# Block-sparse attention and feed-forward kernel: the scores of a row of blocks in two matrix products instead of three, and staging loads in order of use

## The chip, the cores and the metric

The kernel runs on one core of a Trainium2 chip. The metric is the device time of one execution in microseconds. Before the change the median of three runs is 852.0 us (850.26 to 855.06).

## What is computed

Block-sparse attention for 4 batches, 8 heads, 768 positions of 64 elements, and behind it a feed-forward layer with an ELU on the joined heads. A block is 32 positions, so a sequence has 24 blocks. A query sees its own block and both neighbours, the first and the last block, and three sampled blocks; queries of the first and the last block see everything.

```
scores = scale * np.matmul(q, k.transpose(0, 1, 3, 2))
mask = np.abs(blk_i - blk_j) <= 1
mask = mask | (blk_i == 0) | (blk_j == 0) | (blk_i == n_blocks - 1) | (blk_j == n_blocks - 1)
...
attn = np.exp(scores - max); attn = attn / (sum + 1e-09); x = attn @ v
h = x @ w_in
g = np.where(h > 0.0, h, np.exp(np.minimum(h, 0.0)) - 1.0)
out = g @ w_out
```

Inputs q, k and v are float32, the weights float64.

## The kernel before, in words

**Number format.** Every operand of a product is held as a high and a low float16 part, and each product is three float16 products (`PROD`: high x high, high x low, low x high) summed in PSUM.

**Units.** The 22 inner blocks of a batch form six units: `u` 0 to 4 hold four query blocks (`QB`), `u` 5 holds two and, as the "special" rows, the first and the last block. Each unit is done for half of the heads at a time (`qd` 0 and 1; `u` 5 in one go), which makes 11 score units a batch and 44 in all. For each query block a score row has 256 columns (`ROW`): 96 of the window, 32 of the first block, 96 of the sampled blocks, 32 of the last block.

**Scores** (`scores`, L438 to L457). For each head pair half `pp`, each of the three products and each of three parts, there are eight products, four query blocks by two heads. A product takes 64 rows and 32 columns of the array, so the eight cover it. Part 0 reads the window from `kT` (96 columns), part 1 the first and last keys from `kE` (64 columns), part 2 the sampled keys from `kR` (96 columns). A unit is 2 x 3 x 3 x 8 = 144 products, each with its own weight load. `gather_k` (L413 to L420) copies the sampled key blocks of a unit into `kR`, 12 copies on VectorE, whose places it reads from registers; `kR` has one buffer. `ends_of_k` (L370 to L376) fills `kE` once a batch.

**Behind the scores.** `sm_min` (VectorE, with the mask) and `sm_exp` (ScalarE), a step later `sm_hi` and `sm_lo`, then the transpose by DMA on SP's queue (`sm_T`, L500), `attn_v` (L513) four or six steps behind the scores, `norm` (L533) and `turn_x` (transposes on TensorE, L325, and a split into `xT` by ScalarE and VectorE, L313 and L316). The tile `vg` holds the V rows of a unit: the window by SP's queue and the sampled ones by GpSimd's (`gather_v`, L408 and L409), the first and last block by `edge_v` (L400).

**PSUM.** Scores, special scores and the transposes of k, q and x take turns in two buffers (`ps_s`, tag "s"). The special scores take both at once (`sp_scores`, L549) until the exponential (`spt`, L567) is done.

**Feed-forward.** A chunk `t` is two units of a batch, 256 tokens; there are 12. `ffn_h` (L629) is 24 products of 256 columns a step, eight steps a chunk; `ffn_o` (L664) is 12 products of 512 columns a step, eight steps.

**Order.** A table of steps sets the order: `st.at(step, rank, fn)` puts a piece of work in a step, and the pieces are emitted step by step and by rank. A scheduler behind it may still move instructions. Chunk `t` has its feed-forward part at steps 12 + 16t to 28 + 16t; its attention begins 22 steps (`LEAD`) ahead, for chunks 0 and 1 closer. One step of the later chunks is 24 or 12 feed-forward products on TensorE plus, in most steps, a piece of attention. Weights are converted from float64 in 32 pieces by ScalarE, VectorE and GpSimd at steps 2 to 23 (`w_bits1`, `w_sign`, `w_bits2`, `w_split`).

**Staging.** q, k and v of a later chunk or batch come through a ring of three buffers (`st`, `NST`): `load_q`, `load_k`, `load_v` on SP's queue, then `turn_k`, `turn_q` (transposes on TensorE) or `prep_v_hi`, `prep_v_lo` (ScalarE, VectorE), which give the buffer back. Before the change a load of k or v stands two steps ahead of its use, a load of q three; the pieces of k of the next batch are used at steps e0 + 2 + 6n and those of v at e0 + 16 + 4n (n from 0 to 5, e0 the step where the batch's attention begins); for batch 1 they are used at steps 22 to 34, every second step.

Of the kernel before, what the change touches and what calls it, by code (L numbers as in the profile page):

```python
# [7 lines left out]
F32 = mybir.dt.float32  # L8
F16 = mybir.dt.float16
# [5 lines left out]
BLOCK = 32  # L15
# [23 lines left out]
def kernel(  # L39
# [22 lines left out]

    nc = tc.nc
    B, H, S, D = q.shape
    P = 128
# [14 lines left out]
    NFP = NFC // 2  # L82
    CW = 2 * P
    assert D == 64 and NR == 3 and NB == 24 and H == 8

    QS, KS, VS = -2.0, 16.0, 32.0
    SS = 2.0 ** 8
# [73 lines left out]
    mask = const.tile([P, NU, 8], F32, tag="mask", name="mask")  # L161

    def build_mask():
        tb = const.tile([P, 6, 8], F32, tag="tb", name="tb")
# [24 lines left out]
        nc.vector.tensor_scalar(nv[:, 7:8], pq, float(NB - 2), None, op0=ALU.is_equal)  # L189
# [79 lines left out]
    vg = [const.tile([P, 2, QB, H * 2 * D], F16, tag=f"vg{i}", name=f"vg{i}") for i in range(2)]  # L269
    vN = const.tile([P, NK, H, 2, D], F16, tag="vN", name="vN")  # L270
    scr = {}
    kT, qT, kR, kE, stg, nat = {}, {}, {}, {}, {}, {}

    def spare(i, n, m=1):

# [92 lines left out]
                  ps[:, d, 0:P].rearrange("p (a i) -> p a i", a=2), 1.0)  # L368

    def ends_of_k(b):  # L370

        t = work.tile([P, 2 * NPAIR, 2, BLOCK], F16, tag="kE", bufs=1, name=f"kE{b}")
        kE[b] = t
        for e, s0 in enumerate((0, S - BLOCK)):
            nc.vector.tensor_copy(
                t[:, :, e, :], kT[b].rearrange("p l a s -> p (l a) s")[:, :, s0 : s0 + BLOCK])  # L376
# [19 lines left out]
    slot = {}  # L396

    def edge_v(b, s, eng=None):
        for ab, s0 in ((0, 0), (1, S - BLOCK)):
            (eng or nc.sync).dma_start(  # L400
                vg[s][96:P, ab],
                scr[b][s0 : s0 + BLOCK].rearrange("i (o e) -> i o e", o=1).to_broadcast(
                    [BLOCK, QB, H * 2 * D]))

    def gather_v(b, u, i):
        qb = 1 + QB * u + i
# [4 lines left out]
            in_offset=bass.IndirectOffsetOnAxis(ap=rix[0:96, qb : qb + 1], axis=0))  # L411

    def gather_k(b, u):  # L413

        t = work.tile([P, 2 * NPAIR, QB * NR, BLOCK], F16, tag="kR", bufs=1, name=f"kR{b}_{u}")
        kR[b, u] = t
        kk = kT[b].rearrange("p l a s -> p (l a) s")
        for c in range(blocks_in(u) * NR):
            x = token_of(1 + QB * u + c // NR, c % NR)
            nc.vector.tensor_copy(t[:, :, c, :], kk[:, :, bass.ds(x, BLOCK)])  # L420

    def blocks_in(u):
        return QB if u < UL else 2
# [12 lines left out]
    def scores(b, u, qd):  # L436
        ps = ps_s.tile([P, 2, 2, ROW], F32, tag="s", name=f"s{b}_{u}_{qd}")
        pS[b, u, qd] = ps  # L438
        for pp in range(2):
            for ql, kl in PROD:  # L440
                for part in range(3):
                    for n, (d, i, q0) in enumerate(places(u, qd)):
                        a, s0 = 2 * d + pp, BLOCK * (QB * u + i)
                        for j in range(2):
                            js = slice(64 * j, 64 * j + 64)
                            o = ps[32 * n : 32 * n + 32, j, pp, :]
                            if part == 0:
                                o, m = o[:, 0:96], kT[b][js, kl, a, s0 : s0 + 96]
                            elif part == 1:
                                o = o.rearrange("p (a k) -> p a k", a=2)[:, :, 96:128]  # L450
                                m = kE[b][js, kl * NPAIR + a]
                            else:
                                o = o[:, P : P + 96]
                                m = kR[b, u][js, kl * NPAIR + a, NR * i : NR * (i + 1)]
                            nc.tensor.matmul(  # L455
                                o, lhsT=qT[b, u][js, ql, a, q0 : q0 + 32], rhs=m,
                                start=(ql + kl + part == 0), stop=(ql == 1),  # L457
                                skip_group_check=True)

# [234 lines left out]
    def unit(s, b, u, qd, t, c0):  # L694
        lag = 4 if t == 1 else 6
        if qd == 0:
            st.at(s - (3 if t else 1), 3.0, lambda: gather_k(b, u))
        st.at(s, 0, lambda: scores(b, u, qd))
        st.at(s, 5, lambda: sm_min(b, u, qd))
        st.at(s, 6, lambda: sm_exp(b, u, qd))  # L700
        if t == 0:
            st.at(s + 1, 0.5, lambda: turn_p(b, u, qd))
            st.at(s + 2, 1, lambda: attn_v(b, u, qd))
            if qd == 1:
                st.at(s + 2, 3.5, lambda: norm(b, u))
                st.at(s + 3, 0.6, lambda: turn_x(b, u, t, c0))
            return
        st.at(s + 1, 3.1, lambda: sm_hi(b, u, qd))
        st.at(s + 1, 3.2, lambda: sm_lo(b, u, qd))
        st.at(s + 2, 0.5, lambda: sm_T(b, u, qd))  # L710
        a = s + lag
        st.at(a, 1, lambda: attn_v(b, u, qd))
        if u == UL or qd == 1:
            st.at(a, 3.5, lambda: norm(b, u))
            st.at(a, 7, lambda: turn_x(b, u, t, c0))

    def special(s, b, qd, t):
        st.at(s, 0, lambda: sp_scores(b, qd))
# [8 lines left out]
        if qd == NQ - 1:  # L727
            st.at(s + lag, 3.5, lambda: sp_x(b, t, P))

    def k_piece(s, b, c):  # L730
        st.at(s - 2, 0.1, lambda: load_k(b, c))
        st.at(s, 7.2, lambda: turn_k(b, c))

    def v_piece(s, b, g, qd):
        st.at(s - 2, 0.1, lambda: load_v(b, g, qd))
        st.at(s, 3.6, lambda: prep_v_hi(b, g, qd))
        st.at(s, 3.7, lambda: prep_v_lo(b, g, qd))
        if qd == NQ - 1:
            st.at(s + 1, 0.8, lambda: store_v(b, g))

    PIECES = [(g, qd) for g in range(NG) for qd in range(NQ)]
    for t, (b, us) in enumerate(chunks):
# [22 lines left out]
        for m, u in enumerate(us):  # L765
            s = first[m]
            if t == 0:
                continue
            st.at(s - 6, 0.1, lambda b=b, u=u: load_q(b, u))
            st.at(s - 3, 7.1, lambda b=b, u=u: turn_q(b, u))  # L770

        opens = t == 0 or chunks[t - 1][0] < b
        for m, u in enumerate(us):
# [103 lines left out]
```

## Time and profile before

| | |
|---|---|
| median of three runs | 852.0 us |
| the profiled execution, its own time | 850.52 us |
| its span on the core | 848.8 us |
| TensorE products | 716.1 us busy (84%), 15,111 instructions, as many weight loads |
| VectorE, ScalarE, GpSimd | 473.2, 390.9, 270.5 us busy |
| mean granted clock of TensorE | 0.925 |
| score products | three groups of 2,112 |

The profile is of one execution. Busy times overlap, and a share of the whole span mixes stages with different limits, so stretches of the span are read apart. A row of waits names the engine, the tile and the line that waited, what ended the wait, the total in us, how often, and the longest. "issue" means that the profile shows no releaser. A timeline row has start, duration, engine, line, tiles, shapes and count, and in brackets the idle time ahead of it.

### The profile page before, as it was taken

To read this page: it belongs to the slowest core of one execution; us is meant where nothing else is said; L and a number is where in the kernel's file an instruction comes from. 1 tells how busy PE (TensorE), PEld (TensorE's weight loads), DVE (VectorE), ACT (ScalarE), POOL (GpSimd) and SP (SyncE) were. 2 spreads that over 40 slices of the span, in tenths; PEclk is the share of its full clock that TensorE was granted. 3 is DMA by queue.
4 is the path that set the end of the run, shared out by engine and by line. 5 is a ranking of instruction groups with operands and counts; after the bars stand their busy time and mean duration, and the time that the engine had idled before them with its cause. 6 is when DMAs were issued, how large, how long until landed. Compare 5 with 4: busy or idle time off the path is not lost. (4 is left out here: it accounts for less than half of the span.)

```text
span 848.8 us, 34525 instructions
## 1 busy us (share of the span) xinstructions
PE 716.1 (84%) x15111; PEld 497.2 (59%) x15111; DVE 473.2 (56%) x1247; ACT 390.9 (46%) x830; POOL 270.5 (32%) x249
## 2 busy tenths in 40 slices
PE   2355367579699799799899899899999999999998
PEld 2244345337566666666655656757757758567583
DVE  3838789984564664553624664464736635445040
ACT  3542465554543554543534553454635535445140
POOL 1438567730411411412410410421422304213040
PEclk9656759869899899989999999999999999999999
DMA  9995555878749858538638847546868555353000
GB/s 213 319 211 176 162 142 165 200 154 215 179 89 186 157 120 182 127 83 170 126 55 194 162 107 174 128 108 146 141 142 176 86 90 125 47 133 49 29 2 25
DMA packets 204938, 116.59 MB, mean 137 GB/s; under 512 B 163060, under 2 KB 183668, under 8 KB 204788
## 3 DMA queue, kind: packets, MB, share of 16 engines
q1 hardware_dynamic: 191952, 88.89, 50.1%
q0 software_dynamic: 5952, 18.36, 8.4%
q10 hardware_dynamic: 6884, 7.15, 2.8%
q8 instruction: 118, 1.93, 1.0%
q14 instruction: 32, 0.26, 0.1%
HBM read 74.52 MB, written 12.58 MB: 103 GB/s over the span
## 5 line engine op out<-in xcount | busy, mean ns | idle before, releaser
L629 PE MATMUL h<-xT,wih 128*128 128x256 f16 x1536 | 271.4, 282 | 16.3 <-issue 6.2
L664 PE MATMUL o<-woh,g 128*128 128x512 f16 x768 | 242.1, 383 | 5.6 <-ACT woh L263 3.6
L654 POOL TENSOR_TENSOR g<-e,g 128x512 f16<-128x512 f32 x96 | 113.7, 1184 | 364.6 <-DVE g L651 330.4
L629 PE MATMUL h<-xT,wil 128*128 128x256 f16 x768 | 216.3, 282 | 3.1 <-issue 3.1
L664 PEld LDWEIGHTS <-g 128*128 128x128 f16 x1152 | 109.5, 98 | 139.2 <-issue 19.3
L629 PEld LDWEIGHTS <-wih 128*128 128x128 f16 x1536 | 151.5, 101 | 41.5 <-issue 17.5
L664 PE MATMUL o<-wol,g 128*128 128x512 f16 x384 | 147.2, 383 | 6.7 <-POOL wol L264 5.6
L481 ACT ACTIVATE t<-t,m 128x256 f32<-128x256 f32 x176 | 87.3, 497 | 117.1 <-DVE m L466 113.3
L409 POOL DMA_INDIRECT vg<-scr,rix x88 | 84.4, 959 | 133.6 <-PE av L513 113.7
L647 DVE SCALAR_TENSOR_TENSOR e<-h,e 128x512 f32<-128x512 f32 x96 | 66.2, 689 | 72.2 <-ACT e L643 69.3
L466 DVE CUSTOM_DVE_ANT_1 t<-s,mask 128x256 f32<-128x256 f32 x176 | 64.4, 419 | 57.9 <-PE s L455 56.1
L637 ACT ACTIVATE e<-h 128x512 f32<-128x512 f32 x96 | 56.5, 588 | 72.7 <-PE h L629 65.4
L455 PEld LDWEIGHTS <-qT 64*32 64x32 f16 x6336 | 56.5, 91 | 57.1 <-issue 43.5
L629 PEld LDWEIGHTS <-wil 128*128 128x128 f16 x768 | 77.6, 101 | 16.0 <-POOL wx L244 3.1
L493 DVE SCALAR_TENSOR_TENSOR p<-t,p 128x1024 f16<-128x1024 f32 x40 | 48.7, 1218 | 40.4 <-ACT p L488 40.2
L643 ACT ACTIVATE e<-e,gs 128x512 f32<-128x512 f32 x96 | 69.2, 721 | 2.2
L455 PE MATMUL s<-kE,qT 64*32 64x64 f16 x2112 | 57.4, 201 | 15.0 <-issue 11.9
L455 PE MATMUL s<-kR,qT 64*32 64x96 f16 x2112 | 60.8, 215 | 9.3 <-issue 6.7
L455 PE MATMUL s<-kT,qT 64*32 64x96 f16 x2112 | 56.5, 216 | 14.4 <-DVE m L466 10.0
L420 DVE COPY kR<-kT 128x256 f16 x264 | 50.3, 249 | 6.3 <-issue 4.4
L513 PEld LDWEIGHTS <-pT 128*32 128x32 f16 x4224 | 42.6, 98 | 18.7 <-issue 16.2
L513 PE MATMUL av<-vg,pT 128*32 128x64 f16 x4224 | 49.0, 202 | 4.2 <-DMA vg<-scr 3.0
(102 smaller groups left out, 727.3 us busy)
## 6 DMA issues: line engine op xcount, KB each, us to landing
vg<-scr SPq DMA_DIRECT2D x88, 192.0 KB, 5.9
wk<-in_moe_w_out_dram SPq DMA_DIRECT2D x16, 512.0 KB, 3.8
wk<-in_moe_w_in_dram SPq DMA_DIRECT2D x12, 512.0 KB, 4.2
scr<-vN SPq DMA_DIRECT2D x12, 512.0 KB, 4.4
out_dram<-r ACTq DMA_DIRECT2D x20, 256.0 KB, 4.0
stq<-in_q_dram SPq DMA_DIRECT2D x18, 256.0 KB, 4.3
stv<-in_v_dram SPq DMA_DIRECT2D x18, 256.0 KB, 4.2
stk<-in_k_dram SPq DMA_DIRECT2D x18, 256.0 KB, 3.6
```

Source lines behind the costliest of these rows:

```text
L409: nc.gpsimd.indirect_dma_start(out=t[0:96, 1, i], out_offset=None, in_=scr[b], in_offset=bass.IndirectOffsetOnAxis(ap=rix[0:96, qb : qb + ...
L420: nc.vector.tensor_copy(t[:, :, c, :], kk[:, :, bass.ds(x, BLOCK)])
L455: nc.tensor.matmul(o, lhsT=qT[b, u][js, ql, a, q0 : q0 + 32], rhs=m, start=(ql + kl + part == 0), stop=(ql == 1), skip_group_check=True)
L466: nc.vector.tensor_tensor_reduce(t[:, j, pp, :].rearrange("p (a b) -> p a b", b=BLOCK), ps[:, j, pp, :].rearrange("p (a b) -> p a b", b=BL ...
L481: nc.scalar.activation(t[:, j, pp, :], t[:, j, pp, :], AF.Exp, bias=m[:, j, pp : pp + 1], scale=-1.0, accum_out=s[:, h : h + 1])
L513: nc.tensor.matmul(o[32 * n : 32 * n + 32, 4 * qd + 2 * pp + j, :], lhsT=t[:, pl * 8 + (2 * j + pp) * 2 + ab, 32 * n : 32 * n + 32], rhs=v ...
L629: nc.tensor.matmul(ps[:, e, :], lhsT=w[2 * f + e][:, cs], rhs=x[:, l, cc, :], start=(n == 0), stop=(n == 3 * NCC - 1))
L637: nc.scalar.activation(e, hS[t, f], AF.Exp, scale=IH)
L643: nc.scalar.activation(e, e, AF.Relu, bias=gs_col, scale=-GS)
L647: nc.vector.scalar_tensor_tensor(e, hS.pop((t, f)), -IH * GS, e, op0=ALU.mult, op1=ALU.min)
L654: nc.gpsimd.tensor_tensor(gl[f], eS.pop((t, f)), gh[f], op=ALU.subtract)
L664: nc.tensor.matmul(o, lhsT=g[f][:, e, ms], rhs=w[2 * f + e], start=(f == 0 and e == 0 and n == 0), stop=(f == NFP - 1 and e == 1 and n == 2))
```

## The change

- **Two products a row.** `kE` is gone. `kR` is one lasting tile with 17 key blocks in a row: first, three sampled, last, three sampled, first, three sampled, last, three sampled, first. A query block's second product reads five blocks in a row (160 columns) from there: an end, its three sampled blocks, and the other end. For odd query blocks of a unit the last key block comes first and the first one last. So columns 96 to 256 of a row hold the ends in turns, and a unit has 96 products, 48 of 96 columns and 48 of 160.
- **Ends.** `ends_of_k` writes the first keys to three places and the last keys to two, in two copies of 768 and 512 elements a partition. The mask's column for a doubled end moves to match.
- **Edge V.** The end rows of `vg` follow the same order, so `edge_v` issues four DMAs of half the size instead of two: on GpSimd's queue for batch 0 (8 for 4), on SP's for the others (24 for 12).
- **`turn_x`** stands one step later for all chunks but chunk 0.
- **Staging.** Loads are sorted by the step of their use; each is put at the end of a step (rank 9), six steps ahead or at the step in which the third load before it is used, if that is later. For batch 1 that gives leads of two to six steps, from then on always six.
- **K and V pieces** of batches 2 and 3 are used at other steps (K at e0 + 11, 15, 23, 31, 39, 41, V at e0 + 17, 19, 25, 27, 33, 35), none of K between the special scores and their end.
- **`gather_k`** for the first unit of chunk 2 stands one step ahead of its scores instead of three.
- The mask's scratch tile comes from a pool of work tiles.

```diff
-    kT, qT, kR, kE, stg, nat = {}, {}, {}, {}, {}, {}
+    kT, qT, stg = {}, {}, {}
+    kR = const.tile([P, 2 * NPAIR, QB * (NR + 1) + 1, BLOCK], F16, tag="kR", name="kR")
...
     def ends_of_k(b):
-        t = work.tile([P, 2 * NPAIR, 2, BLOCK], F16, tag="kE", bufs=1, name=f"kE{b}")
-        kE[b] = t
-        for e, s0 in enumerate((0, S - BLOCK)):
+        for e, s0 in ((0, 0), (NR + 1, S - BLOCK)):
+            t = kR[:, :, e :: 2 * (NR + 1), :]
             nc.vector.tensor_copy(
-                t[:, :, e, :], kT[b].rearrange("p l a s -> p (l a) s")[:, :, s0 : s0 + BLOCK])
+                t, kT[b].rearrange("p l a s -> p (l a) s")[:, :, s0 : s0 + BLOCK].unsqueeze(2)
+                .to_broadcast([P, 2 * NPAIR, t.shape[2], BLOCK]))
...
     def edge_v(b, s, eng=None):
-        for ab, s0 in ((0, 0), (1, S - BLOCK)):
-            (eng or nc.sync).dma_start(
-                vg[s][96:P, ab],
+        for ab in range(2):
+            for i in range(2):
+                s0 = (S - BLOCK) * (ab ^ i)
+                (eng or nc.sync).dma_start(
+                    vg[s][96:P, ab, i::2],
...
-                for part in range(3):
+                for part in range(2):
...
                             if part == 0:
-                                o, m = o[:, 0:96], kT[b][js, kl, a, s0 : s0 + 96]
-                            elif part == 1:
-                                o = o.rearrange("p (a k) -> p a k", a=2)[:, :, 96:128]
-                                m = kE[b][js, kl * NPAIR + a]
+                                c, m = slice(0, 96), kT[b][js, kl, a, s0 : s0 + 96]
                             else:
-                                o = o[:, P : P + 96]
-                                m = kR[b, u][js, kl * NPAIR + a, NR * i : NR * (i + 1)]
+                                e = (NR + 1) * i
+                                c, m = slice(96, ROW), kR[js, kl * NPAIR + a, e : e + NR + 2]
...
-            st.at(s - (3 if t else 1), 3.0, lambda: gather_k(b, u))
+            st.at(s - (1 if t == 0 or s == F0 + 2 * NSTEP - LEAD else 3), 3.0, lambda: gather_k(b, u))
...
-            st.at(a, 7, lambda: turn_x(b, u, t, c0))
+            st.at(a + 1, 7, lambda: turn_x(b, u, t, c0))
...
+    def q_piece(s, b, u):
+        staged.append((s, lambda: load_q(b, u)))
+        st.at(s, 7.1, lambda: turn_q(b, u))
...
     def k_piece(s, b, c):
-        st.at(s - 2, 0.1, lambda: load_k(b, c))
+        staged.append((s, lambda: load_k(b, c)))
...
-                    k_piece(e0 + 2 + 6 * n, b + 1, n)
-                    v_piece(e0 + 16 + 4 * n, b + 1, g, qd)
+                    k_piece(e0 + (11, 15, 23, 31, 39, 41)[n], b + 1, n)
+                    v_piece(e0 + (17, 19, 25, 27, 33, 35)[n], b + 1, g, qd)
...
+    staged.sort(key=lambda it: it[0])
+    for n, (s, load) in enumerate(staged):
+        st.at(max(s - 6, staged[n - NST][0] if n >= NST else 0), 9, load)
```

TensorE's order where batch 2's second chunk turns its normalised rows (`xt_0` of unit 0, behind a piece `h_4` of the feed-forward part of the chunk before), in the kernel before:

```order
L629 LDWEIGHTS wil_1483
L629 MATMUL h_4_11581<-xT_10021,wil_1483 128x256
L325 MATMUL xt_0_11617<-ident,xf_0_11614 128x128 x4
L325 MATMUL kt_4_11624<-ident,stk_4_11398 128x128 x4
L629 LDWEIGHTS wih_1486
L629 MATMUL h_5_11631<-xT_10021,wih_1486 128x256
```

And now:

```order
L632 LDWEIGHTS wil_1314
L632 MATMUL h_5_10257<-xT_8887,wil_1314 128x256
L331 MATMUL xt_0_10292<-ident,xf_0_10255 128x128 x4
L457 LDWEIGHTS qT_1_9765
L457 MATMUL s_1_1_10301<-kT_5052,qT_1_9765 32x96
```

`xt_0` stood behind `h_4` and had a transpose of k (`kt_4`) right behind it; now it stands behind `h_5`, right ahead of the scores `s_1_1`, and the transpose of k is elsewhere.

SP's queue behind the special scores of batch 2 (`spT`: transposes of the special rows, `pT`: of the others, `stv`, `stk`, `stq`: staging loads, `scr`: V written out, `vg`: V gathered), before:

```order
L588 DMA_TRANSPOSE spT_1_1_10033<-spp_1_1_10014 128x12x128
L293 DMA stv_0_1_10724<-in_v_dram 128x4x128
L500 DMA_TRANSPOSE pT_5_0_10422<-p_5_0_10407 128x16x128
L288 DMA stk_3_10726<-in_k_dram 128x8x64
L306 DMA stq_1_10728<-in_q_dram 128x8x64
L392 DMA scr_11051<-vN 128x2048
L293 DMA stv_1_0_11089<-in_v_dram 128x4x128
L288 DMA stk_4_11398<-in_k_dram 128x8x64
L500 DMA_TRANSPOSE pT_0_0_10730<-p_0_0_10721 128x16x128
```

And now:

```order
L591 DMA_TRANSPOSE spT_1_1_8854<-spp_1_1_8843 128x12x128
L299 DMA stv_0_0_9007<-in_v_dram 128x4x128
L299 DMA stv_0_1_9206<-in_v_dram 128x4x128
L503 DMA_TRANSPOSE pT_5_0_9210<-p_5_0_9195 128x16x128
L312 DMA stq_1_9326<-in_q_dram 128x8x64
L294 DMA stk_2_9466<-in_k_dram 128x8x64
L397 DMA scr_9712<-vN 128x2048
L299 DMA stv_1_0_9611<-in_v_dram 128x4x128
L299 DMA stv_1_1_9773<-in_v_dram 128x4x128
L503 DMA_TRANSPOSE pT_0_0_9468<-p_0_0_9460 128x16x128
```

Pieces 3 and 4 of k stood here, with pieces of v one by one; now it is piece 2 of k, and the pieces of v come in pairs.

More of the change, by code (lines that the diff above doesn't have):

```diff
@@ L84 @@
     assert D == 64 and NR == 3 and NB == 24 and H == 8
+    assert (NB - 3) % QB % 2 == 1
     QS, KS, VS = -2.0, 16.0, 32.0
@@ L163, in build_mask @@
     def build_mask():
-        tb = const.tile([P, 6, 8], F32, tag="tb", name="tb")
+        tb = work.tile([P, 6, 8], F32, tag="e", bufs=NE, name="tb")
         sf, df, t0, t1 = (tb[:, i, :NR] for i in range(4))
@@ L188, in build_mask @@
         nc.vector.tensor_scalar(nv[:, 3:4], pq, 1.0, None, op0=ALU.is_equal)
-        nc.vector.tensor_scalar(nv[:, 7:8], pq, float(NB - 2), None, op0=ALU.is_equal)
+        nc.vector.scalar_tensor_tensor(
+            nv[:, 3:4], pq, float(NB - 2), nv[:, 3:4], op0=ALU.is_equal, op1=ALU.add)
         nb = const.tile([P, 8], BF16, tag="nb", name="nb")
@@ L398, in edge_v @@
     def edge_v(b, s, eng=None):
-        for ab, s0 in ((0, 0), (1, S - BLOCK)):
-            (eng or nc.sync).dma_start(
-                vg[s][96:P, ab],
-                scr[b][s0 : s0 + BLOCK].rearrange("i (o e) -> i o e", o=1).to_broadcast(
-                    [BLOCK, QB, H * 2 * D]))
+        for ab in range(2):
[3 more added lines that the diff above has]
+                    vg[s][96:P, ab, i::2],
+                    scr[b][s0 : s0 + BLOCK].rearrange("i (o e) -> i o e", o=1).to_broadcast(
+                        [BLOCK, QB // 2, H * 2 * D]))
     def gather_v(b, u, i):
@@ L413, in gather_k @@
     def gather_k(b, u):
-        t = work.tile([P, 2 * NPAIR, QB * NR, BLOCK], F16, tag="kR", bufs=1, name=f"kR{b}_{u}")
-        kR[b, u] = t
         kk = kT[b].rearrange("p l a s -> p (l a) s")
-        for c in range(blocks_in(u) * NR):
-            x = token_of(1 + QB * u + c // NR, c % NR)
-            nc.vector.tensor_copy(t[:, :, c, :], kk[:, :, bass.ds(x, BLOCK)])
+        for i in range(blocks_in(u)):
+            for r in range(NR):
+                x = token_of(1 + QB * u + i, r)
+                nc.vector.tensor_copy(
+                    kR[:, :, (NR + 1) * i + 1 + r, :], kk[:, :, bass.ds(x, BLOCK)])
     def blocks_in(u):
@@ L445, in scores @@
                             js = slice(64 * j, 64 * j + 64)
-                            o = ps[32 * n : 32 * n + 32, j, pp, :]
                             if part == 0:
-                                o, m = o[:, 0:96], kT[b][js, kl, a, s0 : s0 + 96]
-                            elif part == 1:
-                                o = o.rearrange("p (a k) -> p a k", a=2)[:, :, 96:128]
-                                m = kE[b][js, kl * NPAIR + a]
-                            else:
-                                o = o[:, P : P + 96]
-                                m = kR[b, u][js, kl * NPAIR + a, NR * i : NR * (i + 1)]
+                                c, m = slice(0, 96), kT[b][js, kl, a, s0 : s0 + 96]
+                            else:
+                                e = (NR + 1) * i
+                                c, m = slice(96, ROW), kR[js, kl * NPAIR + a, e : e + NR + 2]
                             nc.tensor.matmul(
-                                o, lhsT=qT[b, u][js, ql, a, q0 : q0 + 32], rhs=m,
+                                ps[32 * n : 32 * n + 32, j, pp, c],
+                                lhsT=qT[b, u][js, ql, a, q0 : q0 + 32], rhs=m,
                                 start=(ql + kl + part == 0), stop=(ql == 1),
@@ L728, in special @@
             st.at(s + lag, 3.5, lambda: sp_x(b, t, P))
+    staged = []
+    def q_piece(s, b, u):
+        staged.append((s, lambda: load_q(b, u)))
+        st.at(s, 7.1, lambda: turn_q(b, u))
     def k_piece(s, b, c):
-        st.at(s - 2, 0.1, lambda: load_k(b, c))
+        staged.append((s, lambda: load_k(b, c)))
         st.at(s, 7.2, lambda: turn_k(b, c))
     def v_piece(s, b, g, qd):
-        st.at(s - 2, 0.1, lambda: load_v(b, g, qd))
+        staged.append((s, lambda: load_v(b, g, qd)))
         st.at(s, 3.6, lambda: prep_v_hi(b, g, qd))
@@ L768 @@
                 continue
-            st.at(s - 6, 0.1, lambda b=b, u=u: load_q(b, u))
-            st.at(s - 3, 7.1, lambda b=b, u=u: turn_q(b, u))
+            q_piece(s - 3, b, u)
         opens = t == 0 or chunks[t - 1][0] < b
```

## The prediction

> **What bounds the kernel now.** I read the page first, then the stretches with the busy time of each engine, then the waits of TensorE in the two stretches that matter, then the timeline of one score unit.
>
> ```profile
> span 848.8 us, 34525 instructions
> PE 716.1 (84%) x15111; PEld 497.2 (59%) x15111; DVE 473.2 (56%) x1247; ACT 390.9 (46%) x830; POOL 270.5 (32%) x249
> q8 instruction: 118, 1.93, 1.0%
> ```
> ```profile
> core 0: us, PE busy (x) PEld busy (x) DVE busy (x) ACT busy (x) POOL busy (x), PEclk, DMA share, GB/s
> 23.00:80.00 57.00, 25.17 (x1011) 20.03 (x1010) 40.02 (x108) 25.01 (x57) 30.00 (x29) 0.64 0.87 238
> 80.00:196.00 116.00, 73.92 (x1474) 47.62 (x1473) 98.34 (x172) 61.90 (x122) 72.62 (x54) 0.76 0.68 171
> 196.00:650.00 454.00, 418.13 (x9064) 292.06 (x9065) 242.54 (x701) 215.79 (x469) 115.75 (x109) 0.97 0.67 141
> 650.00:848.80 198.80, 191.50 (x3529) 131.44 (x3527) 82.58 (x228) 79.91 (x167) 48.82 (x45) 1.00 0.36 70
> ```
>
> The kernel has two regimes. Up to 196 us TensorE is busy for less than two thirds of a stretch: first the opening attention, then the conversion of the weights on VectorE (98 of 116 us), GpSimd and ScalarE. Behind 196 us TensorE is busy for 610 of 653 us and the next engine for half: what shortens TensorE's work or removes a wait of its own moves the end. Its waits from 196 us on (total, times, longest):
>
> ```profile
> PE xt L325 <- DVE xf L533: 11.8, 5, 6.9
> PE h L629 <- issue: 9.3, 6, 3.3
> PE kt L325 <- ACT spt L567: 7.8, 2, 4.9
> PE s L455 <- issue: 6.3, 8, 1.3
> PE o L664 <- issue: 2.6, 2, 1.6
> PE av L513 <- issue: 0.5, 1, 0.5
> ```
>
> That is 19.6 us for buffers and data (`xt`, `kt`) and 18.7 us of "issue", waits for which the profile shows no releaser.
>
> **The scores, part by part.** The start of one unit at 194.63, and the next unit whole, between products of the feed-forward part (start, duration):
>
> ```profile
> 194.63 0.24 PE L455 MATMUL s<-kT,qT 64*32 64x96 f16 x8 [0.55 <-DVE kT L316]
> ...
> 208.58 0.24 PE L455 MATMUL s<-kT,qT 64*32 64x96 f16 x8
> 208.63 0.21 PE L455 MATMUL s<-kE,qT 64*32 64x64 f16 x8
> 208.66 0.23 PE L455 MATMUL s<-kR,qT 64*32 64x96 f16 x8
> 208.71 0.23 PE L455 MATMUL s<-kT,qT 64*32 64x96 f16 x8
> ...
> 209.62 0.26 PE L455 MATMUL s<-kE,qT 64*32 64x64 f16 x8
> 209.69 0.27 PE L455 MATMUL s<-kR,qT 64*32 64x96 f16 x8
> 209.89 0.39 PE L629 MATMUL h<-xT,wih 128*128 128x256 f16 x2
> ```
>
> Eighteen groups of eight products, each product with a weight load of its own, take 1.31 us. From the first group to the last there are 17 intervals in 1.11 us, 0.065 us each, and late in the unit 64 columns (kE to kR) take the same 0.07 us as 96 do. Only the first groups, which had queued up, follow at 0.05, 0.03, 0.05 us, by their width. So a group costs about 0.065 us for its sixteen instructions, and its columns about 0.03 us per 64. The change leaves twelve groups: six of 96 columns and six of 160. By instructions alone 11 intervals are 0.72 us, plus the 0.20 us to the next product: 0.92, a saving of 0.39. If a wide group costs its columns, 160/64 x 0.03 = 0.075 us, it is 6 x 0.065 + 5 x 0.075 = 0.77, plus 0.20 and 0.03 for a longer last group: 1.00, a saving of 0.31. I take 0.35. Of 44 units nine lie ahead of 196 us or so (four of chunk 0, three of chunk 1, two of chunk 2, whose second is the one at 194.63); 35 x 0.35 = **12 us** (11 to 14).
>
> A rule of the Trainium skill speaks against it (TensorE: Matmul & The Clock Gate, The mechanism): a weight load overlaps a running product only if it goes to another row group. By it the four places of one half of the rows would run one after another, and wider products would cost more than fewer save. Here four 96-column products in a row would need 4 x 0.05 = 0.20 us and a whole group starts every 0.065 us, so the trace doesn't bear the rule out; it is a rival below.
>
> **The waits for xt and kt.** The two stalls for `kt` are transposes of K that stand behind the special scores, which hold both buffers until the exponential is done; no piece of K stands there any more: 7.8 us go. The stalls for `xt` come from VectorE, which does the normalisation behind pieces of V that have not landed. Over the same stretch ScalarE waits:
>
> ```profile
> ACT vN L313 <- DMA stv<-in_v_dram: 39.8, 11, 5.7
> ```
> ```profile
> 226.28 1.11 PE L325 MATMUL xt<-ident,xf 128*128 128x128 f32 x4 [6.88 <-DVE xf L533]
> 227.19 1.06 PE L325 MATMUL kt<-ident,stk 128*128 128x128 f32 x4
> 228.04 0.63 PE L629 MATMUL h<-xT,wih 128*128 128x256 f16 x2
> 228.47 0.42 PE L629 MATMUL h<-xT,wil 128*128 128x256 f16 x1
> ```
>
> Now `turn_x` stands a step later, behind one more piece of 24 products. From batch 1's chunks on, each load is issued six steps ahead. So the four later stalls, 11.8 - 6.9 = 4.9 us, go. The one at 226 us lies where K and V of batch 1 are loaded; there three staging buffers leave leads of two to four steps as before. It shrinks by one step (24 products at 0.11 us, from the 0.43 us below halved to 0.22 per two, 2.6 us) to some 4.2. What is late next at these places is the split of `xt_3`: on VectorE it stands behind the low part of `p_4_1`, and the special scores need its buffer. I allow 1 us at each of three places, **3 us** (0 to 6). Sum: 7.8 + 4.9 + 2.6 - 3 = **12 us**.
>
> Each such stall also leaves TensorE at half clock (granted clock 0.97 on average from 196 to 650 us, 1.00 after): after it two `h` products take 228.47 - 228.04 = 0.43 us, where 0.22 is the rate of undisturbed stretches:
>
> ```profile
> 208.16 0.38 PE L629 MATMUL h<-xT,wih 128*128 128x256 f16 x2
> 208.38 0.27 PE L629 MATMUL h<-xT,wil 128*128 128x256 f16 x1
> ```
>
> I estimate 1 to 2 us lost behind each of the four stalls of 2.8 us or more; with most of them gone, **4 us**.
>
> **The issue waits.** The instruction queue brought 1.93 MB in 118 packets, and 2 x 15,111 instructions of TensorE are most of what is fetched: 1.93 MB / 30,222 is 64 bytes each, so one 16 KB packet is about 256 instructions. A unit's 288 instructions are more than one packet in 1.3 us; 192 are less. TensorE has 4,224 instructions fewer in all (14%). I take half of the 18.7 us, **10 us** with some clock (bounds: 3 by the 14%, 24 if all go). The Trainium skill says the opposite (Runtime: NRT & Kernel Launch, Instruction fetch mechanics): crossing such a block is mostly hidden. By it this term is nothing; that is a rival too.
>
> **The opening.** From 23 to 80 us:
>
> ```profile
> PE s L455 <- issue: 12.7, 3, 5.3
> PE s L455 <- DVE kE L375: 3.1, 1, 3.1
> PE av L513 <- DMA vg<-scr: 3.0, 1, 3.0
> ```
>
> Three stalls inside the score units hold VectorE's minima and everything queued behind them, the weights too. With 384 instructions fewer there I take **5 us** (0 to 12). Against it: the end copies are wider, and edge V takes twice as many issues.
>
> ```profile
> L375 DVE COPY kE<-kT 128x256 f16<-128x256 f16 x8 | 1.5, 215 | 0.0
> ```
> ```profile
> L400 POOL DMA_DIRECT2D vg<-scr x4: 581/604/802, 35.2 to 39.8; - x4
> ```
>
> The copies carry 768 and 512 elements for 256: between 215 ns each and 3 and 2 times that, so 0 to 0.65 us a batch. Only the first pair is waited for (kE, above); elsewhere VectorE is busy for half the time. Four more issues of GpSimd are 2.4 us ahead of its gathers, half of them ahead of the first `av`; twelve more on SP, at that price, are 7 us over the run, with no engine waiting for SP's queue in the lists above. I charge 1 us, inside the 5. The mask takes as many small operations as before, and its scratch tile only comes from another pool: nothing.
>
> **The sum.** 12 + 12 + 4 + 10 + 5 = 43 us, against the profiled execution's own 850.5 us (848.8 of span and 1.7 around it): 807.5. That execution lay 1.5 us under the median of the runs shown, 852.0, so I forecast **809 us** (main case 798 to 821).
>
> **The rivals.**
> - Issue waits stay, because fetches are bound by other traffic, in the opening too: 850.5 - 12 - 12 - 4 = 822.5, as a median **824**. For it: the waits fall on `h` and `o` as well, where instructions are sparse. Chance 0.17.
> - The `xt` and `kt` stalls come back elsewhere, since three staging buffers are all there is: 850.5 - 12 - 10 - 5 = 823.5, **825**. Against it: from 650 us, where no K and V are loaded, none is left. 0.10.
> - The edit doesn't do what it says: a 160-column group costs as much as the two it replaces, and only the order gains: 850.5 - 12 - 4 - 10 - 5 = 819.5, **821**. 0.05.
> - All stalls go: 14 for the scores, 19.6 and 4, 24, 10: 779, **780**. 0.08.
> - Slower: loads on SP. A load that waits for a staging buffer holds the transposes of p behind it, and `av` waits for those.
>
> ```profile
> SPq L308 <- PE kt L325: 16.3, 3, 10.2
> ```
> ```profile
> 304.46 3.42 SPq L500 DMA_TRANSPOSE pT<-p  x1
> 317.80 1.01 PE L513 MATMUL av<-vg,pT 128*32 128x64 f16 x96
> ```
> ```profile
> pT<-p SPq DMA_TRANSPOSE x40, 5.5
> ```
>
> The transpose lands 5.5 us after issue and has 317.8 - 304.5 = 13.3, so 7.8 us cover a held queue. The longest hold seen is 10.2; if each of the 22 units of batches 1 and 2 met it, 2.4 x 22 = 53 us would come on top: 807.5 + 53, as a median **862**. It ends above the present time from holds of 9.8 us at every unit. Against it: six steps ahead, the buffer has been given back by the load's place in the program. 0.04.
> - Slower: the places of one row half run one after another. A unit is 6 x 4 x (0.05 + 0.075) = 3.0 us, 1.7 more than now; 35 x 1.7 = 59 us for a saving of 12: 807.5 + 12 + 59, **880**. The trace refutes it for today's widths. That is what the rule of the Trainium skill named above (TensorE: Matmul & The Clock Gate, The mechanism) would do. 0.02.
>
> **How the numbers follow.** The main case has 0.54. The range 788 to 831 takes it in with the first three rivals, and leaves out the fast end and both slow cases, 0.14, and some of the main case's tail. A measurement of this kernel can tell 0.5%, about 4 us, from no change: faster by more than that are the main case and the first four, 0.92, less some for unforeseen stalls: 0.90; the slow cases and those, 0.06; the rest 0.04.
>
> **What would show it.** In the changed profile: 96 products a unit, first to next `h` in 0.9 to 1.0 us; no `kt` wait on `spt`, the `xt` waits under 6 us; issue waits of TensorE behind the opening about half of 18.7; the three stalls of the opening under 8 us together. The prediction is wrong if units take over 1.1 us, if `av` waits for transposes, or if the special scores wait for `xt_3` by more than 2 us each.

## The result, and the profile after

| | kernel before | changed kernel |
|---|---|---|
| median of the runs | 851.2 us (850.26 to 855.06, 4 runs) | 790.67 us (788.61 to 794.8, 4 runs) |
| the profiled execution, its own time | 850.52 us | 794.8 us |
| its span | 848.8 us | 792.7 us |
| mean granted clock of TensorE | 0.925 | 0.931 |

The changed kernel takes 0.9285 of the time [0.9254, 0.9316]: 60 us less, where 43 were forecast. The head of the page, with the instruction queue, and the two groups that are left of the scores:

```profile
span 792.7 us, 30338 instructions
PE 693.7 (88%) x12999; PEld 480.9 (61%) x12999; DVE 480.4 (61%) x1247; ACT 387.7 (49%) x830; POOL 272.9 (34%) x253
q8 instruction: 102, 1.67, 0.9%
L457 PE MATMUL s<-kT,qT 64*32 64x96 f16 x2112 | 45.5, 217 | 20.8 <-issue 8.1
L457 PE MATMUL s<-kR,qT 64*32 64x160 f16 x2112 | 48.7, 250 | 5.8 <-DVE kR L425 5.0
```

TensorE lost 2,112 products and as many weight loads, and 22 us of busy time; the span lost 56 us. So most of the gain was idle time of TensorE. The stretches show where (each row: window, its length, then busy time and instructions of PE, PEld, DVE, ACT and POOL, granted clock, DMA share, GB/s):

```profile
23.00:80.00 57.00, 25.80 (x828) 19.51 (x827) 38.71 (x110) 25.04 (x57) 32.80 (x33) 0.61 0.84 235
80.00:190.00 110.00, 75.66 (x1242) 47.82 (x1241) 101.31 (x178) 62.87 (x125) 73.56 (x54) 0.74 0.69 182
190.00:600.00 410.00, 396.21 (x7789) 278.03 (x7788) 245.94 (x698) 211.69 (x467) 113.30 (x108) 0.99 0.70 155
600.00:792.70 192.70, 188.78 (x3110) 129.75 (x3107) 84.79 (x224) 79.86 (x168) 49.94 (x46) 1.00 0.36 74
```

Behind 190 us TensorE is now busy for 585 of 603 us, where it was 610 of 653, and its granted clock in the long stretch rose from 0.97 to 0.99. Its waits from 190 us to the end (total, times, longest):

```profile
PE xt L369 <- DVE xf L536: 4.5, 2, 2.7
PE s L457 <- DVE xT L322: 2.6, 2, 1.4
PE h L632 <- DVE e L650: 2.1, 1, 2.1
PE h L632 <- issue: 1.6, 1, 1.6
PE kt L331 <- DVE kT L322: 1.1, 1, 1.1
PE s L457 <- DVE kR L379: 0.5, 1, 0.5
PE xt L331 <- DVE xf L536: 0.5, 1, 0.5
PE sp L552 <- DVE xT L322: 0.4, 2, 0.2
PE av L516 <- issue: 0.3, 1, 0.3
PE s L457 <- issue: 0.2, 1, 0.2
```

The waits for `kt` behind `spt` are gone, those for `xt` are 5.0 us instead of 11.8, and "issue" is 2.1 us instead of 18.7. One unit between products of the feed-forward part, in its timeline:

```profile
200.92 0.24 PE L457 MATMUL s<-kT,qT 64*32 64x96 f16 x8
200.97 0.25 PE L457 MATMUL s<-kR,qT 64*32 64x160 f16 x8
201.04 0.23 PE L457 MATMUL s<-kT,qT 64*32 64x96 f16 x8
201.08 0.25 PE L457 MATMUL s<-kR,qT 64*32 64x160 f16 x8
201.16 0.27 PE L457 MATMUL s<-kT,qT 64*32 64x96 f16 x8
...
201.63 0.29 PE L457 MATMUL s<-kR,qT 64*32 64x160 f16 x7
201.85 0.39 PE L632 MATMUL h<-xT,wih 128*128 128x256 f16 x2
```

From its first group to the next `h` it is 201.85 - 200.92 = 0.93 us, against 1.31. The eleven intervals between the starts of its twelve groups add up to 0.71 us, 0.065 us each on average, as before. They are not alike: in the medians of 33 units of this trace, the next group starts 0.075 us behind a group of 160 columns, and 0.058 us behind a group of 96 once the unit has settled. A pair takes 0.133 us, as two groups of the kernel before do, at 0.067 us each.

Set against the span, 848.8 - 792.7 = 56.1 us:

| term | forecast | measured | from |
|---|---|---|---|
| 35 score units | 12 | 13 | 35 x (1.31 - 0.93) |
| waits for `xt`, `kt` and what came in their place | 12 | 8.5 | 20.2 (19.6, and 0.55 at `s`) less 11.7 |
| issue waits behind the opening | 10 | 17 | 18.7 less 2.1 |
| clock behind the stalls | 4 | 9, an estimate | 454 us x (1 - 0.97/0.99) |
| opening and weights | 5 | 7.5 | the second unit of chunk 2 starts at 187.09 us, not 194.63 |

The measured column gives 55 us. The first three and the last are differences of rows; the clock is not separated from them by any run. The trace's records of the granted clock give the same size for it: behind the opening TensorE was busy for 24.5 us at half clock before and is for 6.5 us now, and half of the difference is 9 us.

```profile
187.09 0.31 PE L457 MATMUL s<-kT,qT 64*32 64x96 f16 x8
```

### The profile page after: what moved, and what is told of

Same layout as the page of the kernel before. It is cut to its first block, busy times and chain, and to the rows that moved or that the text cites. A ratio compares the mean times of both kernels' runs of the same rounds, so it can differ in the third digit from the quotient of the medians.

```text
span 792.7 us, 30338 instructions
## 1 busy us (share of the span) xinstructions
PE 693.7 (88%) x12999; PEld 480.9 (61%) x12999; DVE 480.4 (61%) x1247; ACT 387.7 (49%) x830; POOL 272.9 (34%) x253
## 4 chain that ended last, share of the span: by engine, by line
PE 55%; DMA 3%; DVE 3%; ACT 3%; issue 1%; SPq 0%; DVEq 0%; ACTq 0%
PE h L632 24%; PE o L667 21%; PE s L457 4%; PE av L516 4%; DMA stv<-in_v_dram 3%; ACT t L484 1%; PE qt L331 1%; PE xt L331 1%; DVE p L496 1%; PE sp L552 1%; ACT p L491 1%; DVE vN L322 1%; DVE e L650 1%; PE kt L331 0%; PE spx L603 0%
## 5 line engine op out<-in xcount | busy, mean ns | idle before, releaser
L632 PE MATMUL h<-xT,wih 128*128 128x256 f16 x1536 | 266.0, 280 | 14.9 <-DVE e L650 6.2
L457 PEld LDWEIGHTS <-qT 64*32 64x32 f16 x4224 | 41.8, 94 | 39.6 <-issue 29.5
L457 PE MATMUL s<-kT,qT 64*32 64x96 f16 x2112 | 45.5, 217 | 20.8 <-issue 8.1
L425 DVE COPY kR<-kT 128x256 f16 x264 | 52.9, 251 | 10.8 <-PE s L457 5.6
L457 PE MATMUL s<-kR,qT 64*32 64x160 f16 x2112 | 48.7, 250 | 5.8 <-DVE kR L425 5.0
L654 DVE CAST g<-e 128x512 f16<-128x512 f32 x96 | 51.7, 539 | 2.7
L516 PEld LDWEIGHTS <-pT 128*32 128x32 f16 x4224 | 41.5, 96 | 14.9 <-issue 11.9
L516 PE MATMUL av<-vg,pT 128*32 128x64 f16 x4224 | 47.3, 199 | 1.6 <-ACT pT L319 1.1
```

What stands on the lines that cost most here:

```text
L457: nc.tensor.matmul(ps[32 * n : 32 * n + 32, j, pp, c], lhsT=qT[b, u][js, ql, a, q0 : q0 + 32], rhs=m, start=(ql + kl + part == 0), stop=(q ...
L516: nc.tensor.matmul(o[32 * n : 32 * n + 32, 4 * qd + 2 * pp + j, :], lhsT=t[:, pl * 8 + (2 * j + pp) * 2 + ab, 32 * n : 32 * n + 32], rhs=v ...
L632: nc.tensor.matmul(ps[:, e, :], lhsT=w[2 * f + e][:, cs], rhs=x[:, l, cc, :], start=(n == 0), stop=(n == 3 * NCC - 1))
```

## The experiments

Each diff stands against the changed kernel. "Issue" and "other waits" are TensorE's from 190 us to the end; the kernel before has 18.7 (without a row of 0.3 us at `kt`) and 20.2 us, the changed kernel 2.1 and 11.7.

**The products alone.** The order, the steps and the leads of before, with two products a row:

```diff
-            st.at(a + 1, 7, lambda: turn_x(b, u, t, c0))
+            st.at(a, 7, lambda: turn_x(b, u, t, c0))
-                    k_piece(e0 + (11, 15, 23, 31, 39, 41)[n], b + 1, n)
-                    v_piece(e0 + (17, 19, 25, 27, 33, 35)[n], b + 1, g, qd)
+                    k_piece(e0 + 2 + 6 * n, b + 1, n)
+                    v_piece(e0 + 16 + 4 * n, b + 1, g, qd)
...
-        staged.append((s, lambda: load_k(b, c)))
+        st.at(s - 2, 0.1, lambda: load_k(b, c))
...
-            st.at(s - (1 if t == 0 or s == F0 + 2 * NSTEP - LEAD else 3), 3.0, lambda: gather_k(b, u))
+            st.at(s - (3 if t else 1), 3.0, lambda: gather_k(b, u))
```

> The change's two products a row in the order of the kernel before (turn_x, loads and pieces of K and V where they were). Burst theory: the issue waits behind the opening come from runs of TensorE instructions longer than one fetched block of about 256, so 192 instead of 288 removes them: issue waits under 5 us, the waits for xt and kt near 20 us as before, units 0.38 us shorter, about 812 us. Order theory: the issue waits went because the loads are spread differently; then they stay near 18 us here and the time is about 828 us.

In this kernel the sampled keys of unit 5 of batch 0 are overwritten by the next unit's before its scores read them; the instructions are the same in number and size. It took 823.43 us (821.92 to 824.02), 0.9684 of before [0.9638, 0.9731]. Its waits from 190 us:

```profile
PE xt L331 <- DVE xf L536: 18.9, 8, 5.2
PE kt L331 <- ACT spt L570: 8.3, 2, 5.1
PE o L667 <- issue: 1.5, 1, 1.5
```

With 0.3 us more at `av` the issue waits are 1.8 us, as the burst theory has them. The time lies between the two theories' figures, since the waits for `xt` have grown.

The same with `gather_k` where the change has it:

> Two products a row alone, as e1_scores_only, but with gather_k of the first unit of chunk 2 one step ahead of its scores, so that no unit reads keys of another. Time as e1 (0.968 of the kernel before, about 824 us); issue waits behind the opening under 3 us, xt waits about 20 us.

It took 819.67 us (817.37 to 821.05), 0.962 [0.9582, 0.9657], with 18.4 us at `xt`, 8.2 at `kt` and 5.1 of issue, where under 3 and 0.968 were expected. So fewer products, in an unchanged order, take most of the issue waits away and are worth 27 to 32 us; the waits for `xt` grow from 11.8 us, since TensorE comes to them earlier and VectorE doesn't.

**The order alone.** The changed kernel with three products a row again, the ends read from `kR`:

```diff
-                for part in range(2):
+                for part in range(3):
...
+                            elif part == 1:
+                                e = (NR + 1) * i
+                                m = kR[js, kl * NPAIR + a, e : e + NR + 2 : NR + 1]
...
-                                c, m = slice(96, ROW), kR[js, kl * NPAIR + a, e : e + NR + 2]
+                                c, m = slice(P, P + 96), kR[js, kl * NPAIR + a, e + 1 : e + NR + 1]
```

> The changed kernel with three products a row again (96, 64 and 96 columns, from the same kR), all else as changed. Burst theory: issue waits return to 15 to 20 us behind the opening, xt and kt waits stay low, a unit takes 1.38 us again; 13 us of units, 17 of issue waits, some 5 of clock and 3 to 5 in the opening on top of 791: about 828 us. Order theory: issue waits stay near 2 us, about 806 us.

It took 827.56 us (823.29 to 832.54), 0.9734 [0.9666, 0.9802]. A unit takes 1.38 us from its first start to its last end, as before, and the issue waits are back:

```profile
PE h L637 <- issue: 6.5, 3, 4.4
PE h L637 <- DVE e L655: 5.5, 3, 2.6
PE s L462 <- issue: 4.8, 7, 1.4
PE xt L369 <- DVE xf L541: 1.5, 2, 1.0
```

12.5 us of issue, against 2.1, though not the 15 to 20 that were expected: the new order takes the waits for `xt` and `kt`, the products take most of those for instructions.

**Where the issue waits come from.** The prediction took a packet of 256 instructions as the unit of fetching. The timeline of before shows it more sharply than I had read it:

```profile
337.12 0.39 PE L629 MATMUL h<-xT,wih 128*128 128x256 f16 x2 [0.41 <-issue]
...
338.86 0.24 PE L455 MATMUL s<-kT,qT 64*32 64x96 f16 x8
...
339.77 0.21 PE L455 MATMUL s<-kR,qT 64*32 64x96 f16 x1
341.12 0.23 PE L455 MATMUL s<-kR,qT 64*32 64x96 f16 x7 [1.14 <-issue]
```

Between the two stalls lie 15 products of `h`, then 14 groups of eight and one more of the scores: 128 products with their loads, 256 instructions, and the stall falls inside a group of eight. Counted through the whole trace of before, the 23 stalls of over 0.15 us lie 255, 128, 383, 1022, 512, 637, 2043, 128, 383, 894, 384, 638, 128, 383, 383, 1278, 1022, 511, 639, 895, 384 and 894 products apart: multiples of 128, less 0 to 5. With the boundaries placed by these stalls, the blocks of 256 that end behind 196 us sort by the time that TensorE took for one, its closing stall left out:

| kernel | blocks under 4 us | stalls at their end | blocks of 4 us or more | stalls |
|---|---|---|---|---|
| before | 16 | 11, 14.0 us | 83 | 7, 4.9 us |
| changed | 0 | none | 85 | 2, 1.9 us |
| order alone | 15 | 10, 11.9 us | 84 | 2, 0.6 us |

So most stalls follow where 256 instructions run out in less than about 4 us, which a unit of 288 does and one of 192 with feed-forward products around it doesn't. The changed kernel's third wait for instructions, 0.2 us at `s`, lies at no such boundary.

The trace also records the packets of the instruction queue (`q8`), 16,384 bytes each. All 23 stalls of before end 1.3 to 1.7 us after such a packet has landed, so what TensorE waits for is the next block of instructions. In the kernel before, two packets never start less than 3.4 us apart, while the shortest block runs out in 1.24 us. The seven stalls behind blocks of 4 us or more have late packets: they start 2.7 to 5.2 us after TensorE entered that block, where the median of all blocks behind 190 us is 1.2 us. What made them late no run shows. Two kernels try whether the burst makes the stalls.

A unit of three products in two runs of 72, feed-forward products between them:

```diff
-        st.at(s, 0, lambda: scores(b, u, qd))
+            st.at(s, 0, lambda: scores(b, u, qd, 0))
+            st.at(s, 2.05, lambda: scores(b, u, qd, 1))
```

> As e2_three_products, but from chunk 2 on a unit's 144 products stand in two runs of 72 with a step's feed-forward products between them; the instruction count is that of e2. Burst theory: issue waits behind the opening at 6 us or less, time 12 to 20 us under e2, less some 7 us for 37 more changes between narrow and wide products (0.2 us each): 813 to 820 us. Count theory (the waits follow the number of instructions fetched): issue waits as in e2, time 5 to 8 us above e2.

839.61 us (832.6 to 842.67), 0.9893 [0.9843, 0.9943]: slower than the order alone, with 8.2 us of issue and 13.1 of `xt`. No block is shorter than 3.6 us any more; of the 15 under 4 us one stalls (0.4 us), but of the 26 of 4 to 5 us six do (7.0 us), each with a packet that starts 2.0 to 3.8 us after TensorE entered the block. So 4 us is no sharp bound. The fewer issue waits fit the theory, their number and the time miss it, and splitting a unit moves other work as well: in the profiled executions, 3.2 us apart, the waits for `xt` grow from 1.5 us by more than the issue waits lose. This run decides nothing.

The other way about, short bursts joined with no instruction added: `attn_v` of units 0 to 3 (96 products, from chunk 3 on) right behind the scores of a later unit:

```diff
-        lag = 4 if t == 1 else 6
+        lag, near = (4, False) if t == 1 else (6, False)
+        if t > 2 and u < 4:
+            lag, near = 8, True
...
-        st.at(a, 1, lambda: attn_v(b, u, qd))
+        st.at(a, 0.1 if near else 1, lambda: attn_v(b, u, qd))
```

> The changed kernel with attn_v of the units 0 to 3 from chunk 3 on two steps later, right behind the scores of the unit after next: runs of 384 TensorE instructions at many places, with no instruction more. Burst theory: blocks of 256 instructions are again run through in under 4 us, and issue waits behind the opening come back, 7 us or more (from 2.1), with some clock: 799 to 808 us. Count theory: issue waits stay under 4 us, 789 to 796 us.

813.6 us (810.48 to 820.74), 0.9571 [0.9489, 0.9654]. Its waits, and one of them in the timeline, inside the `attn_v` behind a unit's scores:

```profile
PE av L516 <- issue: 13.7, 7, 2.5
PE h L632 <- issue: 3.2, 3, 1.7
```
```profile
331.81 0.69 PE L516 MATMUL av<-vg,pT 128*32 128x64 f16 x47
334.60 0.29 PE L516 MATMUL av<-vg,pT 128*32 128x64 f16 x14 [2.11 <-issue]
```

16.9 us of issue against 2.1, with the same instructions in another order: 14 blocks under 4 us now, ten of them with a stall, 16.9 us, and no stall at the 71 others. Each of these stalls, too, ends 1.3 to 1.6 us after an instruction packet has landed. That is the burst, and not the number of instructions, which is the same. The time lies above what was expected, though: 23 us over the changed kernel by the medians, 19 by the spans, of which the issue waits are 15 and the other waits less than 2. TensorE is busy for 13.6 us at half clock behind the opening, against 6.5; half of the difference, 3.6 us, is an estimate of what the clock adds, and makes up the 19 us of the spans.

**`turn_x` in its old step.**

```diff
-            st.at(a + 1, 7, lambda: turn_x(b, u, t, c0))
+            st.at(a, 7, lambda: turn_x(b, u, t, c0))
```

> The changed kernel with turn_x back in the step of attn_v. If the later turn_x is what took the xt waits away, they come back: 10 us or more behind the opening, 799 us or more. If the earlier loads did it (the prediction's reason for the four later stalls), xt waits stay under 6 us but for the place of the first loads, and the time is within 3 us of the changed kernel.

809.64 us (803.74 to 810.99), 0.9533 [0.9487, 0.958].

```profile
PE xt L331 <- DVE xf L536: 17.8, 10, 5.2
PE xt L369 <- DVE xf L536: 3.1, 2, 2.8
```

The waits for `xt` are 20.9 us against 5.0, and the time is 19 us longer by the medians (9 by the spans of the two profiled executions, 802.0 and 792.7; this kernel's was its shortest, the changed kernel's its longest). All other waits together are 21.5 us against 11.7, since waits that the changed kernel has at `s` and `h` are gone here.

**The loads at their old leads**, two steps for k and v, three for q:

```diff
-        staged.append((s, lambda: load_v(b, g, qd)))
+        st.at(s - 2, 0.1, lambda: load_v(b, g, qd))
```

> The changed kernel with loads issued as before: k and v two steps ahead of their use, q three, at the start of the step. If the later turn_x took the xt waits away (theory), the leads are worth little: xt waits under 7 us, 788 to 797 us. If the leads did it (the prediction's reason), xt waits of 10 us or more come back: over 800 us.

791.65 us (791.0 to 792.22), 0.93 [0.9241, 0.936]: not to be told from the changed kernel's 0.9285. Its waits for `xt` are even less:

```profile
PE xt L369 <- DVE xf L536: 0.3, 1, 0.3
```

**The pieces of K and V in their old steps.**

```diff
-                    k_piece(e0 + (11, 15, 23, 31, 39, 41)[n], b + 1, n)
-                    v_piece(e0 + (17, 19, 25, 27, 33, 35)[n], b + 1, g, qd)
+                    k_piece(e0 + 2 + 6 * n, b + 1, n)
+                    v_piece(e0 + 16 + 4 * n, b + 1, g, qd)
```

> The changed kernel with the pieces of K and V of batches 2 and 3 used at the old steps. Theory: the waits of kt for the special exponential come back, about 8 us and some 2 us of clock: 800 us. Rival: with shorter units and the later turn_x they are hidden: within 3 us of 791.

807.04 us (805.28 to 809.39), 0.9488 [0.9424, 0.9553].

```profile
PE kt L331 <- ACT spt L570: 10.0, 2, 5.2
PE qt L331 <- DVE xT L322: 5.8, 2, 3.0
```

Moving them is worth 16 us. The wait for `kt` accounts for 10. The transposes of q (`qt`) wait another 5.8 at two other places, 77 us behind those of `kt`, and there it is a piece of V: ScalarE waits for its load, VectorE for ScalarE, the split of `xT` stands behind VectorE's part of it, and `qt` needs the buffer.

```profile
341.49 0.63 ACT L319 ACTIVATE vN<-stv 128x512 f16<-128x512 f32 x1 [8.05 <-DMA stv<-in_v_dram]
343.12 0.69 DVE L322 SCALAR_TENSOR_TENSOR xT<-xt,xT 128x512 f16<-128x512 f32 x1 [0.21 <-ACT xT L319]
343.87 0.66 PE L331 MATMUL qt<-ident,stq 128*128 128x128 f32 x4 [2.86 <-DVE xT L322]
```

**Products and the later `turn_x`, without the pieces and the leads** (both edits above together):

> Two products a row and turn_x a step later alone; leads and pieces of K and V as before. Theory: these two carry the change but for the kt waits: issue waits about 2 us, xt waits under 8, kt waits about 8, 800 us. If leads and pieces carry more together than one by one, 808 us or more.

807.59 us (803.44 to 811.18), 0.9499 [0.9434, 0.9565], with 10.3 us at `kt`, 5.3 at `qt` and 1.0 of issue. It agrees with the kernel that keeps the new leads, 807.04.

**`turn_x` of unit 5 one step later still**, with the old leads, in search of a better version:

```diff
-            st.at(a + 1, 7, lambda: turn_x(b, u, t, c0))
+            st.at(a + (2 if u == UL and t > 1 else 1), 7, lambda: turn_x(b, u, t, c0))
```

> The changed kernel with the old leads (which cost nothing) and turn_x of unit 5 one more step later from chunk 3 on, since its transposes still waited for the normalisation, 4.5 us in two places of the changed profile. Theory: these waits go, 786 to 789 us. Rival: they were made by that one execution (in e5_old_leads they are 0.3 us): within 0.5% of the changed kernel.

789.22 us (786.5 to 790.5, 6 runs), 0.9259 [0.923, 0.9288]. Its waits for `xt` are 0.3 us, but others take their place (3.0 us at `s`, 2.3 at `kt`), and the intervals overlap: no gain that this measurement can tell.

## Why the prediction was right, and where it was wrong

In the order in which the parts were laid on each other, by the medians: 851 before; 820 to 823 with the products alone; 808 with the later `turn_x`; 791 with the pieces in new steps; 791 with the loads as well. The forecast of 809 us held the sign and, but for the loads, the mechanism. The time lies in its range by only 2.7 us, and below its main case of 798 to 821: four of the five terms came out larger than forecast, and the issue waits went nearly as far as in the rival in which all stalls go (780 us, chance 0.08). The chances of the main case and the first four rivals add up to 0.94, not 0.92. Point by point:

- **Scores: right.** 0.38 us a unit, against 0.35 taken and the instruction-bound end of 0.39. A pair of groups costs its instructions, 0.133 us; within it the wide group takes 0.075 us, the price by width, and the narrow one makes up for it with 0.058. So the rivals in which wide groups cost as much as two, or the places of one row half run one after another, are out. By the rule of the Trainium skill (TensorE: Matmul & The Clock Gate, The mechanism) a weight load overlaps a product only if it goes to another row group; the timeline above, where groups of 96 and 160 columns start 0.05 and 0.07 us apart, doesn't agree with it for these 64-by-32 tiles.
- **Issue waits: the mechanism right, the size wrong.** The term was half of 18.7 us; 17 went. I had the packet of 256 instructions and the 288 of a unit side by side, and then took "half" for want of a rule. The rule was in the trace: the stalls lie a multiple of 128 products apart, and most follow blocks that ran in under 4 us. With 192 instructions a unit there are no such blocks. That would have led towards the upper bound. The rival in which the waits stay is out, by the products alone and by the joined bursts; its reason, other traffic, is not tested for the late packets. The Trainium skill (Runtime: NRT & Kernel Launch, Instruction fetch mechanics) has these crossings mostly hidden; of the 99 blocks of before in the table 18 ended in a stall, 19 us in all, so the trace agrees for most of the slow blocks and not for the fast ones.
- **`xt`: near in sum, 8.5 us for 12 with `kt`, wrong in its reason.** The step that failed is "from batch 1's chunks on, each load is issued six steps ahead. So the four later stalls go". With the old leads the stalls are gone as well; with `turn_x` in its old step they are back, 20.9 us. What removed them is the step of feed-forward products that now lies ahead of the transposes, at all places and not only at 226 us. The loads gained nothing, since they aren't really earlier: from 190 us on each goes out within 6 us of the same time in both kernels, where four steps would be over 10 us. At 280 us they stand on SP's queue behind the transposes of the special rows, which wait for VectorE. The queue there in the changed kernel; the same loads with the old leads; SP's waits for VectorE ahead of these transposes, and ScalarE's waits for V, 38.0 us where they were 39.8, both behind the opening:

```profile
275.82 3.96 SPq L591 DMA_TRANSPOSE spT<-spp  x2
279.88 7.51 SPq L299 DMA_DIRECT2D stv<-in_v_dram  x2
```
```profile
280.68 5.67 SPq L299 DMA_DIRECT2D stv<-in_v_dram  x2
```
```profile
SPq L591 <- DVE spp L585: 33.8, 10, 7.5
ACT vN L319 <- DMA stv<-in_v_dram: 38.0, 11, 7.1
```

- **`kt`: right, too small.** The forecast took the 7.8 us of the waits themselves. With the pieces in their old steps and all else as changed they are 10.0, with 5.8 more at `qt` from the pieces of V. A stall's price read from the trace of before isn't its price once the other stalls are gone.
- **`xt_3`: right in size, at another place.** I allowed 3 us for the special scores waiting on its split; they wait 0.4, but ordinary scores wait 2.6 us for a split of `xT` on VectorE.
- **Clock: too small.** 4 us taken; the granted clock puts it at about 9, an estimate. I had counted the stalls of 2.8 us or more for `xt` and `kt`, and not those for instructions, of which two are over 3 us long. In the kernel before, six half-clock stretches behind the opening, 31 us together, stand at these six stalls, one each. Not every such stall has one: with the products alone a wait of 3.5 us for `xt` has none.
- **Opening: about right**, 7.5 for 5; in the stretch from 23 to 80 us the issue waits fell from 12.7 to 8.1 us, where under 8 had been named. The wait for `kR`, with the wider copies in its place, is 5.0 us, for 5.5 at `kE` and `kR` together:

```profile
PE s L457 <- issue: 8.1, 2, 5.3
PE s L457 <- DVE kR L425: 5.0, 3, 3.7
```

- **The slower rival on SP's queue** didn't come: no wait of `av` for a transpose is among TensorE's.

What stays open: the clock's share by itself, since no run holds it apart from the stalls; what made some instruction packets late; why the joined bursts are 23 us slower by the medians, where 20 are accounted for; and why two short bursts did worse than one long one by 12 us of the medians.

## What to carry to other kernels

Count the instructions of a burst of small products against the block of 256 in which they were fetched here, and look whether the engine runs through one faster than the next arrives (3.4 us from packet to packet at the least here); fewer or wider products, or slower work between, then save more than their own time. Where an engine waits for a late producer, move the consumer a step behind other work, and price each stall as it stands once the others are gone. Judge the lead of a load by when its queue issues it, not by its step in the program.

## What the runs showed of the hardware that was not expected

- In the kernel before, TensorE's stalls without a releaser lie at multiples of 256 instructions, up to 5.3 us each in the opening and up to 3.3 us behind it, and each ends 1.3 to 1.7 us after an instruction packet has landed; joining two bursts with no instruction more brought 15 us of them back.
- On 64-by-32 tiles a group of eight products with its eight loads starts 0.067 us behind the one before at 64 and at 96 columns; with 160 and 96 columns in turns a pair takes the same 0.133 us, 0.075 of it behind the wide group.
